# Regrouping the first MLP matmul, moving weight loads, and moving one layernorm from VectorE to ScalarE in a two-layer spectral and MLP kernel

## The chip, the cores and the metric

The kernel runs on one core of a Trainium2 chip. The metric is the time on the device in microseconds (us), as the median of several executions. The kernel before takes 796.93 us (5 runs, 795.81 to 799.64).

The engines are TensorE (PE in the profile, its weight loads PEld), VectorE (DVE), ScalarE (ACT), GpSimd (POOL), and SyncE (SP), which only issues transfers here. Each works through its own instructions in order.

## The reference, cut to what matters

```
def _A_ref(x, w_r, w_i):                     # spectral mixer, S = 2048, D = 576
    X = rfft2(x.astype(float32))             # over sequence and features
    return irfft2(X * (w_r + 1j * w_i), s=(S, D)).astype(bfloat16)

def _B_ref(x, w1, b1, w2, b2):               # MLP, F = 4608
    h = gelu(layernorm(x) @ w1 + b1)
    return h @ w2 + b2

x = A_x                                      # (1, 2048, 576) bf16
for _ in range(2):                           # two layers, same weights
    x = x + _A_ref(layernorm(x), A_w_r, A_w_i)
    x = x + _B_ref(layernorm(x), B_w1, B_b1, B_w2, B_b2)
```

## The kernel before

The Fourier transforms are matmuls with constant matrices. `x` stays in SBUF, the memory that the engines work from, as 16 tiles of 128 x 576. Matmuls write to PSUM; an *eviction* is the copy from PSUM to SBUF. Transforms of the layer's input come first (the change doesn't touch them), then these stages:

- **Inner stage** (`middle`): 16 steps of transform, multiplication by the spectral weights, and transform back. Each result `h` goes through an SBUF-to-SBUF transfer, the *exchange*, to other partitions. The next stage needs all 16 of them.
- **Output stage** (`spectral_out`): eight steps of two tiles. It also normalises and transposes ("turns") the first quad of four tiles for the MLP (`Prep`).
- **MLP**: four quads of four tiles. Each has a first matmul (`mlp_up`, with GELU) and a second one (`mlp_down`).

PSUM has three buffers of two banks (`big_ps`), handed out in turn. The parts that the change touches:

```
# inner stage: four buffers in turn for what the exchange sends
h = at(r_sb, [P, 2, KP], 592 * (10 + n % 4))
if n % 4 == 2: nc.vector.tensor_copy(out=h[:], in_=ph[:, :, 0:KP])
else:          nc.scalar.copy(out=h[:], in_=ph[:, :, 0:KP])
exchange(hx, E_ORDER[n], h)

# output stage
for n in range(9):
    if n < 8:
        idft_v(n)                 # 8 matmuls, then ScalarE evicts u2(n)
        if n % 2 == 0: idft_v_rest(n // 2)
    if n >= 1: idft_k(n - 1)      # two tiles: 6 matmuls each, 3 VectorE adds each
    if n == 2: prep.stats()       # VectorE statistics, ScalarE square root, VectorE reciprocal
    if 3 <= n < 7: prep.norm(n - 3)          # VectorE
    if 4 <= n < 8: prep.turn(n - 4, "act")   # 5 transposes, ScalarE eviction
    ...

# first MLP matmul: D = 576 is four 128-row pieces and one of 64 rows
for fg in range(0, NFC, 4):       # NFC = 36 chunks of 128 hidden features
    phs = [big_ps([P, 2, 512]) for _ in range(2)]
    for q in range(4):
        for ci in range(4):       # 16 full-height matmuls
            nc.tensor.matmul(phs[q // 2][:, q % 2, :], lhsT=w1_sb[...], rhs=yT[:, ci, :], start=(ci == 0), stop=False)
    for q in range(4):            # 4 half-height ones, two at a time in the two halves of the array
        rows = slice(64 * (q % 2), 64 * (q % 2) + 64)
        nc.tensor.matmul(phs[q // 2][:, q % 2, :], lhsT=w1r_sb[rows, ...], rhs=yT[rows, 4, :], start=False, stop=True)
    ...                           # four GELU evictions on ScalarE
```

In layer 1 the weights `w1` are loaded during the inner stage (three loads of 576 KB) and the output stage (the rest).

## Time and profile before

Stage lengths in the profiled execution run from a stage's first matmul to the next stage's first:

| Stage | Layer 1, us | Layer 2, us |
|---|---|---|
| inner | 33.19 | 29.52 |
| output | 33.52 | 33.36 |
| first MLP matmul, each of 4 passes | 36.86 | 36.86 to 36.88 |
| second MLP matmul, 4 passes | 41.16 to 52.13 | 35.45 to 36.41 |

The second MLP matmul of layer 1 is long because layer 2's input transforms run within it, and after it in its last pass (52.13 us).

The head of the page, three rows of busy time in 40 slices (tenths; PEclk is the TensorE clock that was granted, in tenths of full speed), and the chain of waits:

```profile
span 795.4 us, 12427 instructions
...
PE   8877799999999999999998787999999999999998
...
ACT  7944355433543354335423734552064125303610
...
PEclk9999899999999999999999998999999999999999
...
PE 79%; DVE 7%; issue 5%; DMA 4%; ACT 2%; POOL 1%; SPq 0%; POOLq 0%; ACTq 0%; DVEq 0%
```

TensorE is 79% of the chain. It has few gaps in the MLP passes; the sevens and eights are the spectral stages with their input transforms, and the two dips of the clock fall in the output stages.

The first MLP matmul, from the timeline of TensorE (start us, length us, engine, line, operation, count):

```profile
511.46 0.61 PE L529 MATMUL psb<-yT,w1r_sb 64*128 64x512 bf16 x4
512.00 3.63 PE L523 MATMUL psb<-yT,w_sb 128*128 128x512 bf16 x16
515.55 0.60 PE L529 MATMUL psb<-yT,w1r_sb 64*128 64x512 bf16 x4
516.09 0.39 PE L523 MATMUL psb<-yT,w_sb 128*128 128x512 bf16 x1
```

A group of four chunks repeats every 4.10 us. The starts of the single matmul records show where it goes:

```
full-height   515.028   515.243              steps of 0.216 us
half-height   515.555 (with 515.558)         0.312 after the last full-height one
half-height   515.782 (with 515.784)         0.227 later
full-height   516.093                        0.311 later
```

Each change between full and half height costs about 0.095 us on top of the 0.216 us that a matmul takes anyway.

Waits in layer 1's inner stage that end with a transfer (engine, line, waited-for: total us, times, longest):

```profile
ACT r_sb L407 <- DMA b_sb<-r_sb: 6.4, 6, 1.8
...
DVE r_sb L405 <- DMA b_sb<-r_sb: 2.6, 2, 1.4
```

L407 and L405 are the evictions into the four `h` buffers. They wait for the exchange to have read the buffer's old content.

Layer 2's output stage, from the timeline of ScalarE (in brackets: idle before, and what ended it), and, in the second fence, the longest of TensorE's waits there:

```profile
473.42 0.58 ACT L449 CAST u2r<-pss 34x512 bf16<-34x512 f32 x1
480.21 0.30 ACT L259 ACTIVATE sq<-mv,c_eps 128x4 f32<-128x4 f32 x1 [6.21 <-DVE mv L252]
480.53 1.01 ACT L436 CAST u<-psb 128x1024 bf16<-128x1024 f32 x1
```

```profile
PE psb L431 <- ACT u L436: 4.2, 1, 4.2
```

The square root (L259) stands in ScalarE's queue behind VectorE's statistics and holds up the eviction of `u` (L436) behind it; TensorE then waits 4.2 us for that PSUM buffer. The clock pays afterwards. The stretch from 480.3 to 487.1 (window and length; busy us of PE, PEld, DVE, ACT, POOL, with counts; granted clock; DMA):

```profile
480.30:487.10 6.80, 5.51 (x36) 3.53 (x36) 4.51 (x10) 3.31 (x5) 0.24 (x1) 0.50 0.01 2
```

The granted clock is 0.50. The Trainium skill (TensorE: Matmul & The Clock Gate, Part 1) says that TensorE's clock goes to half after an idle window of about 3.4 us. This trace agrees only in part: the half-clock stretch lasts 6.8 us, two such windows, but it begins 2.9 us into the gap of 4.2 us (477.40 to 481.59).

The four spectral stages in the same view, in order of time:

```profile
43.89:77.08 33.19, 23.71 (x143) 14.01 (x144) 23.59 (x69) 17.01 (x28) 6.01 (x10) 0.95 0.61 177
77.08:110.60 33.52, 26.60 (x244) 19.02 (x245) 26.35 (x60) 16.69 (x22) 5.36 (x11) 0.90 0.35 107
436.82:466.34 29.52, 22.29 (x143) 13.34 (x143) 23.12 (x68) 16.81 (x28) 1.25 (x2) 1.00 0.47 138
466.34:499.70 33.36, 26.53 (x244) 18.98 (x245) 26.26 (x60) 16.69 (x22) 0.94 (x4) 0.90 0.00 1
```

In the output stages (second and fourth line) VectorE is busy 26.3 us, ScalarE 16.7 us, and the clock is 0.90.

### The profile page before, as it was taken

How to read it: one execution, taken by the hardware profiler on the slowest of the kernel's cores; microseconds unless marked ns; L12 is line 12 of the kernel's file. 1: busy time of each engine (PE TensorE's matmuls, PEld its weight loads, DVE VectorE, ACT ScalarE, POOL GpSimd, SP SyncE). 2: the span in 40 equal slices, each digit the busy share in tenths (PEclk: the TensorE clock that was granted, in tenths of full speed). 3: DMA queues.
4: the chain of work that ended last, by engine and by line, in shares of the span. 5: the costliest groups of instructions: out<-in, count | busy, mean ns of one | idle time of the engine just before them, and what ended most of it. 6: DMA issues, size and time to landing. Idle time of an engine off the chain costs nothing.

```text
span 795.4 us, 12427 instructions
## 1 busy us (share of the span) xinstructions
PE 751.7 (95%) x5195; PEld 460.1 (58%) x5195; DVE 272.4 (34%) x865; ACT 330.5 (42%) x512; POOL 46.7 (6%) x89
## 2 busy tenths in 40 slices
PE   8877799999999999999998787999999999999998
PEld 5644553686368536863685545338735853684376
DVE  7765790136013601340142958601220140010011
ACT  7944355433543354335423734552064125303610
POOL 3220111000000000000004000100000000000000
PEclk9999899999999999999999998999999999999999
DMA  8855337000000000000004510430000000000000
GB/s 245 223 155 165 106 103 240 1 10 15 0 9 9 16 1 8 8 16 1 8 15 141 149 47 1 153 116 9 23 1 1 16 16 1 8 16 8 0 9 22
DMA packets 19079, 41.58 MB, mean 52 GB/s; under 512 B 1860, under 2 KB 12944, under 8 KB 19024
## 3 DMA queue, kind: packets, MB, share of 16 engines
q0 software_dynamic: 7040, 27.88, 11.6%
q1 hardware_dynamic: 11584, 12.46, 5.2%
q8 instruction: 40, 0.66, 0.3%
q10 hardware_dynamic: 400, 0.47, 0.2%
q14 instruction: 15, 0.12, 0.0%
HBM read 28.93 MB, written 2.36 MB: 39 GB/s over the span
## 4 chain that ended last, share of the span: by engine, by line
PE 79%; DVE 7%; issue 5%; DMA 4%; ACT 2%; POOL 1%; SPq 0%; POOLq 0%; ACTq 0%; DVEq 0%
PE psb L551 35%; PE psb L523 32%; PE psb L529 5%; DMA b_sb<-r_sb 2%; PE psb L309 2%; DVE tt L467 1%; PE psb L461 1%; PE psb L431 1%; POOL h_sb L201 1%; PE pss L510 1%; DVE x_sb L468 1%; PE pss L299 1%; ACT u L436 1%; DMA h_sb<-const_i 1%; DVE x_sb L469 1%
## 5 line engine op out<-in xcount | busy, mean ns | idle before, releaser
L523 PE MATMUL psb<-yT,w_sb 128*128 128x512 bf16 x1152 | 261.0, 380 | 1.3 <-DVE x_sb L469 1.3
L536 ACT ACTIVATE h_sb<-psb,b_sb 128x512 bf16<-128x512 f32 x288 | 174.5, 688 | 200.9 <-PE psb L529 200.9
L551 PEld LDWEIGHTS <-h_sb 128*128 128x128 bf16 x2304 | 223.2, 98 | 58.2 <-issue 3.4
L523 PEld LDWEIGHTS <-w_sb 128*128 128x128 bf16 x1152 | 107.3, 98 | 148.3 <-issue 28.1
L551 PE MATMUL psb<-r_sb,h_sb 128*128 128x288 bf16 x1280 | 168.9, 286 | 0.0
L551 PE MATMUL psb<-v_sb,h_sb 128*128 128x288 bf16 x1024 | 133.7, 286 | 0.0
L559 DVE TENSOR_TENSOR x_sb<-psb,xb 128x576 bf16<-128x576 f32 x32 | 24.2, 758 | 260.5 <-PE psb L551 260.5
L500 DVE TENSOR_SCALAR xn<-x_sb,mv,rs 128x576 bf16<-128x576 bf16 x32 | 12.8, 426 | 198.4 <-PE pss L510 141.1
L251 DVE BATCH_NORM_STATS2 stats<-x_sb 128x6 f32<-128x288 bf16 x128 | 50.9, 440 | 0.0
L512 ACT COPY yT<-pss 128x640 bf16<-128x640 bf16 x32 | 22.2, 692 | 65.0 <-PE pss L510 65.0
L301 ACT COPY xT<-pss 96x768 bf16<-96x768 bf16 x32 | 25.2, 788 | 45.0 <-PE pss L299 45.0
L529 PE MATMUL psb<-yT,w1r_sb 64*128 64x512 bf16 x288 | 43.6, 381 | 0.0
L314 ACT ACTIVATE z<-psb,rs 128x580 bf16<-128x580 f32 x32 | 29.5, 921 | 20.8 <-PE psb L309 20.5
L503 POOL COPY xn<-xn 128x64 bf16<-128x64 bf16 x32 | 7.6, 248 | 426.5 <-DVE xn L500 351.2
L467 DVE TENSOR_TENSOR tt<-psb,x_sb 128x576 f32<-128x576 f32 x32 | 24.0, 750 | 20.7 <-PE psb L461 20.7
L309 PE MATMUL psb<-c_fd,xT 96*128 96x290 bf16 x192 | 30.1, 292 | 0.5 <-ACT y L330 0.4
L461 PE MATMUL psb<-c_gd,u 128*128 128x288 bf16 x128 | 27.2, 306 | 3.3 <-ACT u L436 1.7
L330 ACT CAST y<-psb 128x580 bf16<-128x580 f32 x24 | 15.4, 640 | 32.3 <-PE psb L327 32.3
L378 ACT CAST r_sb<-psb 128x580 bf16<-128x580 f32 x32 | 20.4, 643 | 20.0 <-PE psb L376 9.8
L402 PE MATMUL psb<-r_sb,h_sb 128*128 128x290 bf16 x128 | 21.9, 291 | 7.1 <-DVE r_sb L390 3.9
L529 PEld LDWEIGHTS <-w1r_sb 64*128 64x128 bf16 x288 | 8.2, 94 | 30.5 <-issue 30.5
L547 DVE TENSOR_TENSOR xb<-x_sb,b_bc 128x576 f32<-128x576 bf16 x32 | 24.0, 749 | 0.0
(80 smaller groups left out, 534.2 us busy)
## 6 DMA issues: line engine op xcount, KB each, us to landing
r_sb<-in_B_w_dram POOLq DMA_DIRECT2D x4, 1440.0 KB, 7.4
w_sb<-in_B_w_dram POOLq DMA_DIRECT2D x8, 576.0 KB, 5.4
v_sb<-in_B_w_dram POOLq DMA_DIRECT2D x4, 1152.0 KB, 6.8
h_sb<-const_i POOLq DMA_DIRECT2D x8, 384.0 KB, 6.0
v_sb<-y SPq DMA_DIRECT2D x16, 145.0 KB
b_sb<-r_sb SPq DMA_DIRECT2D x16, 145.0 KB
b_sb<-y SPq DMA_DIRECT2D x16, 145.0 KB
v_sb<-r_sb SPq DMA_DIRECT2D x16, 145.0 KB
```

The lines of the kernel that those rows point to most:

```text
L251: nc.vector.bn_stats(out=stats[:, h, :], in_=x_sb[:, t, h * DH : (h + 1) * DH])
L301: marks["turn", t] = nc.scalar.copy(out=xT[:], in_=pt[0:96]).ins
L309: nc.tensor.matmul(pz[:, o, 0:KP], lhsT=xT[:, 3 * o + ci, :], rhs=c_fd[:, 3 * o + ci, :], start=(ci == 0), stop=(ci == 2),)
L314: nc.scalar.activation(out=z[:].rearrange("p r (j o) -> p r o j", o=2), in_=pz[:, :, 0:KP].rearrange("p o (r j) -> p r o j", r=2), func=AC ...
L461: nc.tensor.matmul(po[:, o, 0:DH], lhsT=lhsT, rhs=c_gd[0 : (98 if q == 2 else 128), 3 * o + q, :], start=(q == 0), stop=(q == 2),)
L467: nc.vector.tensor_tensor(out=tt[:], in0=po[:, 0:1, 0:DH].to_broadcast([P, 2, DH]), in1=xr, op=ALU.add)
L523: nc.tensor.matmul(phs[q // 2][:, q % 2, :], lhsT=w1_sb[:, ci, (fg + q) * 128 : (fg + q + 1) * 128], rhs=yT[:, ci, :], start=(ci == 0), st ...
L529: nc.tensor.matmul(phs[q // 2][:, q % 2, :], lhsT=w1r_sb[rows, (fg + q) // 2, :], rhs=yT[rows, 4, :], start=False, stop=True,)
L536: marks["ht", fc] = nc.scalar.activation(out=ht[:], in_=phs[q // 2][:, q % 2, :], func=ACT.Gelu_apprx_tanh, bias=b1_sb[:, fc : fc + 1], sc ...
L547: nc.vector.tensor_tensor(out=xb[:], in0=xr, in1=b2_bc[:].rearrange("p (h n) -> p h n", h=2), op=ALU.add)
L551: nc.tensor.matmul(po[:, h, 0:DH], lhsT=hts[fc][:, i * 128 : (i + 1) * 128], rhs=w2_chunk[fc][:, h * DH : (h + 1) * DH], start=(fc == 0), ...
L559: nc.vector.tensor_tensor(out=xr, in0=po[:, :, 0:DH], in1=xb[:], op=ALU.add)
```

## The change

It has three parts, each for one stage:

1. **First MLP matmul.** Six chunks share one visit to half-height mode instead of four. The third pair of chunks starts its sum with the half-height matmuls and adds the full-height ones afterwards. All three PSUM buffers are used.
2. **Inner stage.** Nine `h` buffers instead of four, and in layer 1 three `w1` loads move into the output stage.
3. **Output stage.** Statistics and norms of the first quad go from VectorE to ScalarE, spread over more steps. The sums of `x` and of its square come from two ScalarE passes per tile with an accumulator output. The turns come later.

```diff
-            h = at(r_sb, [P, 2, KP], 592 * (10 + n % 4))
+            h = at(r_sb, [P, 2, KP], 592 * (10 + n % 9))
 [...]
-            if n == 2:
-                prep.stats()
-            if 3 <= n < 7:
-                prep.norm(n - 3)
-            if 4 <= n < 8:
-                prep.turn(n - 4, "act")
+            if n == 2:
+                prep.stats_act((0, 1))
+            if n == 3:
+                prep.stats_act((2, 3))
+            if n == 4:
+                prep.scale_act()
+            for i in {5: (0, 1), 6: (2,), 7: (3,)}.get(n, ()):
+                prep.norm_act(i)
+            for i in {6: (0,), 7: (1, 2), 8: (3,)}.get(n, ()):
+                prep.turn(i, "act")
 [...]
+        def stats_act(self, tiles):
+            [...]
+            for i in tiles:
+                t = self.quad[i]
+                for k, func in enumerate((ACT.Copy, ACT.Square)):
+                    nc.scalar.activation(out=at(h_sb, [P, D], 512 * 34), in_=x_sb[:, t, :], func=func, accum_out=sums[:, k, i : i + 1])
+        def scale_act(self):
+            [... mean and variance from the sums: three small VectorE operations ...]
+            nc.scalar.activation(out=var[:], in_=var[:], func=ACT.Sqrt, bias=c_eps[:, 1:2], scale=1.0 + EPS)
+            nc.vector.reciprocal(out=rs[:], in_=var[:])
+            [... shift = -mean * rs ...]
+        def norm_act(self, i):
+            [...]
+            nc.scalar.activation(
+                out=xn[:, 0:D], in_=x_sb[:, self.quad[i], :], func=ACT.Identity, bias=shift[:, i : i + 1], scale=rs[:, i : i + 1]
+            )
+            nc.gpsimd.tensor_copy(out=xn[:, D:640], in_=xn[:, D - 64 : D])
 [... mlp_up: the old loop over groups of four is replaced by: ...]
+        for p in range(0, NFC // 2, 3):          # p counts pairs of chunks
+            for k in range(2):
+                acc[p + k] = big_ps([P, 2, 512])
+                full(p + k, True)                # 8 full-height matmuls, start the sum
+            acc[p + 2] = big_ps([P, 2, 512])
+            for k in range(3):
+                rest(p + k, k == 2)              # 2 half-height ones; they start the third pair's sum
+            gelu(p)
+            gelu(p + 1)
+            full(p + 2, False)                   # end the third pair's sum
+            gelu(p + 2)
 [... loads of layer 1, inner stage ...]
-                6: [lambda b: load_w1(0, 0, b)],
-                8: [lambda b: load_w1(1, 0, b)],
-                10: [lambda b: load_w1(2, 0, b)],
 [... loads of layer 1, output stage ...]
-                1: [lambda: load_w1(3, 0, t0), lambda: load_w1r(0, t0), lambda: load_w1r(1, t0)],
+                0: [lambda: load_w1(0, 0, ("u2", 0)), lambda: load_w1(1, 0, ("u2", 0))],
+                1: [lambda: load_w1(2, 0, t0), lambda: load_w1(3, 0, t0)],
+                2: [lambda: load_w1r(0, t0), lambda: load_w1r(1, t0)],
```

More of the change, by code (lines that the diff above doesn't have):

```diff
@@ L402, in idft_c @@
                     nc.tensor.matmul(ph[:, o, 0:KP], lhsT=i1[:, n % 4, pl, :], rhs=xp[:, ri, :], start=(q == 0), stop=(q == 1))
-            h = at(r_sb, [P, 2, KP], 592 * (10 + n % 4))
+            h = at(r_sb, [P, 2, KP], 592 * (10 + n % 9))
             if n % 4 == 2:
-                nc.vector.tensor_copy(out=h[:], in_=ph[:, :, 0:KP])
+                ins = nc.vector.tensor_copy(out=h[:], in_=ph[:, :, 0:KP]).ins
             else:
-                nc.scalar.copy(out=h[:], in_=ph[:, :, 0:KP])
+                ins = nc.scalar.copy(out=h[:], in_=ph[:, :, 0:KP]).ins
+            marks["h", n] = ins
             exchange(hx, E_ORDER[n], h)
@@ L435, in idft_v @@
             u2 = work.tile([P, 2, 2, 2, 128], BF16, tag="turn")
-            nc.scalar.copy(out=u2[:], in_=pu[:])
+            marks["u2", n] = nc.scalar.copy(out=u2[:], in_=pu[:]).ins
             st["u2", n] = u2
@@ L491, in __init__ @@
             self.quad, self.st, self.sqrt = QUADS[q], {}, sqrt
+        def stats_act(self, tiles):
+            if 0 in tiles:
+                self.sums = work.tile([P, 2, 4], F32, tag="ln_sums", name=f"sums{uid()}")
+            sums = self.sums
+            for i in tiles:
+                t = self.quad[i]
+                for k, func in enumerate((ACT.Copy, ACT.Square)):
+                    nc.scalar.activation(out=at(h_sb, [P, D], 512 * 34), in_=x_sb[:, t, :], func=func, accum_out=sums[:, k, i : i + 1])
+            self.sums = sums
+        def scale_act(self):
+            s1, s2 = self.sums[:, 0], self.sums[:, 1]
+            mean = work.tile([P, 4], F32, tag="ln_hv")
+            var = work.tile([P, 4], F32, tag="ln_v")
+            rs = work.tile([P, 4], F32, tag="ln_rs", bufs=4)
+            shift = work.tile([P, 4], F32, tag="ln_t")
+            nc.vector.tensor_scalar(out=mean[:], in0=s1, scalar1=1.0 / D, scalar2=None, op0=ALU.mult)
+            nc.vector.tensor_mul(out=shift[:], in0=mean[:], in1=mean[:])
+            nc.vector.scalar_tensor_tensor(out=var[:], in0=s2, scalar=1.0 / D, in1=shift[:], op0=ALU.mult, op1=ALU.subtract)
+            nc.scalar.activation(out=var[:], in_=var[:], func=ACT.Sqrt, bias=c_eps[:, 1:2], scale=1.0 + EPS)
+            nc.vector.reciprocal(out=rs[:], in_=var[:])
+            nc.vector.scalar_tensor_tensor(out=shift[:], in0=mean[:], scalar=-1.0, in1=rs[:], op0=ALU.mult, op1=ALU.mult)
+            self.rs_shift = rs, shift
+            self.yT = work.tile([P, 5, 512], BF16, tag="yT", bufs=1, name=f"yT{uid()}")
+        def norm_act(self, i):
+            rs, shift = self.rs_shift
+            xn = work.tile([P, 640], BF16, tag="xn", bufs=3)
+            nc.scalar.activation(
+                out=xn[:, 0:D], in_=x_sb[:, self.quad[i], :], func=ACT.Identity, bias=shift[:, i : i + 1], scale=rs[:, i : i + 1]
+            )
+            nc.gpsimd.tensor_copy(out=xn[:, D:640], in_=xn[:, D - 64 : D])
+            self.st[i] = xn
         def stats(self):
@@ L518, in mlp_up, with full, rest, gelu @@
         loads = list(loads)
-        for fg in range(0, NFC, 4):
-            phs = [big_ps([P, 2, 512]) for _ in range(2)]
-            for q in range(4):
+        acc = {}
+        def full(p, first):
+            ph = acc[p]
+            for q in range(2):
+                fc = 2 * p + q
                 for ci in range(4):
                     nc.tensor.matmul(
-                        phs[q // 2][:, q % 2, :], lhsT=w1_sb[:, ci, (fg + q) * 128 : (fg + q + 1) * 128], rhs=yT[:, ci, :],
-                        start=(ci == 0), stop=False,
-                    )
-            for q in range(4):
-                rows = slice(64 * (q % 2), 64 * (q % 2) + 64)
-                nc.tensor.matmul(
-                    phs[q // 2][:, q % 2, :], lhsT=w1r_sb[rows, (fg + q) // 2, :], rhs=yT[rows, 4, :],
-                    start=False, stop=True,
-                )
-            for q in range(4):
-                fc = fg + q
+                        ph[:, q, :], lhsT=w1_sb[:, ci, fc * 128 : (fc + 1) * 128], rhs=yT[:, ci, :],
+                        start=(first and ci == 0), stop=(not first and ci == 3),
+                    )
+        def rest(p, first):
+            for q in range(2):
+                rows = slice(64 * q, 64 * q + 64)
+                nc.tensor.matmul(acc[p][:, q, :], lhsT=w1r_sb[rows, p, :], rhs=yT[rows, 4, :], start=first, stop=not first)
+        def gelu(p):
+            for q in range(2):
+                fc = 2 * p + q
                 ht = at(h_sb, [P, 512], 512 * fc)
                 marks["ht", fc] = nc.scalar.activation(
-                    out=ht[:], in_=phs[q // 2][:, q % 2, :], func=ACT.Gelu_apprx_tanh, bias=b1_sb[:, fc : fc + 1], scale=1.0
+                    out=ht[:], in_=acc[p][:, q, :], func=ACT.Gelu_apprx_tanh, bias=b1_sb[:, fc : fc + 1], scale=1.0
                 ).ins
                 hts.append(ht)
+        for p in range(0, NFC // 2, 3):
[9 more added lines that the diff above has]
+            gelu(p + 2)
             if loads:
-                loads.pop(0)(("ht", fg))
+                loads.pop(0)(("ht", 2 * p))
         return hts
```

## The prediction

> **What bounds it now.** The chain of waits is 79% TensorE: the eight MLP passes (first matmul 32%, second 35%) run back to back at granted clock 1.00. The spectral stages do not. In the table of busy time by stretch, layer 1's inner transforms take 33.5 us (43.5 to 77.0), layer 2's only 29.8; each spectral output stage takes 33.4 us with TensorE busy 26.5 us, VectorE 26.3 us, ScalarE 16.7 us, and clock 0.90.
>
> **1. MLP first matmul (eight passes of nine groups).** In the timeline a group of four chunks takes 4.096 us: 18 matmul slots of 0.2158 us = 3.884, the rest is the step from full-height to half-height matmuls (0.312 instead of 0.216 us, so 0.096 lost), the step back (0.095), and about 0.02 of small gaps. The Trainium skill (TensorEngine Tiling, Key Properties) says that a change of tiling mode drains TensorE; this trace agrees, about 0.095 us each. The change makes six groups of six chunks: 27 x 0.2158 + about 0.22 = 6.05 us, 36.3 instead of 36.9 us a pass. All of it is critical: 8 x 0.56 = **4.5 us**. The third PSUM buffer should cause no waits: GELUs start every 0.605 us, so a buffer is free about 0.8 us before it is needed.
>
> **2. Layer 1's inner transforms.** Evictions and VectorE copies there wait for the exchange transfers (waits: 6.4 + 2.6 us, landing up to 7 us late), since w1 loads share the DMA engines and only four buffers exist. Nine buffers and no w1 loads remove both. VectorE then paces it as in layer 2 (1.31 us an iteration, about 0.7 more in every fourth; last eviction to next matmul 3.1 us): out stage starts near 73.3 instead of 77.1: **3.7 us**. Layer 2's inner transforms do not change.
>
> **3. Spectral output, both layers.** VectorE needs 1.52 us per tile; the next matmul's PSUM buffer needs 14 tiles, 21.3 us. Before, it also does statistics (3.85 us) and four norms (1.8 us), and ScalarE's square root waits in order for the statistics (idle until 480.2), holding the next eviction and TensorE for 4 us; the clock then falls to half for 6.8 us (480.3 to 487.1). Moving the work to ScalarE adds there eight passes of 128x576 (estimate 0.65 us each, from the 0.54 us spacing of 128x580 evictions plus bias pointer), four norms (about 0.8), and delays evictions. The Trainium skill (ScalarE: Activation LUTs, What ACT_TABLE_LOAD costs) gives about 93 ns for each pointer operand. Working through the new order with these durations, the first MLP matmul comes about 28.5 us after the stage's start, not 33.4, provided that the clock stays full: 4.7 us each, **9.4 us** in all. No table load is added. w1's loads, now in this stage, need about 21 us from its start and are there in time.
>
> Sum 17.6 us: **779.5 us**, range 774.5 to 786.5. Faster by over 2%: 0.60; within 2%: 0.39; slower: 0.01.
>
> **What shows it.** Six half-height matmuls in a row and 36.3 us a pass; no waits of evictions for the exchange in layer 1; output stages of about 28.7 us with ScalarE busier than 24 us, VectorE below 23 us, and clock near 1.0.
>
> **What would make it wrong.** Accumulating activations that cost far more than 0.65 us, or the strict order on ScalarE holding evictions, so that the output stage gains under 3 us; half clock staying; w1 arriving late for the first MLP pass; exchange transfers still backlogged at the end of layer 1's inner transforms by the remaining loads.

## The result, and the profile after

The changed kernel takes 781.83 us (8 runs, 780.94 to 784.01). The kernel before took 797.54 us in the same rounds and those above (15 runs). The ratio is 0.9807, with a 95% interval of 0.9794 to 0.9821. A ratio is the mean time of one kernel's fast runs over that of the other's of the same rounds, so it is not quite the ratio of the medians. The change is worth 1.9%; the interval straddles the 2% line, so whether it is "faster by over 2%" stays unclear.

The page's head, the same rows and the chain:

```profile
span 779.6 us, 12441 instructions
...
PE   8877899999999999999998787999999999999998
...
ACT  7954865324542454236323658551164126303600
...
PEclk9999999999999999999999999999999999999999
...
PE 81%; DVE 5%; ACT 5%; issue 5%; DMA 3%; POOL 1%; SPq 0%; ACTq 0%; POOLq 0%; DVEq 0%
```

In this execution the clock no longer dips, and ScalarE's share of the chain has grown from 2% to 5%. The span went from 795.4 to 779.6 us; the stages account for the 15.8 us:

| Stage | Before, us | After, us | Difference | Predicted |
|---|---|---|---|---|
| first MLP matmul, sum of 8 passes | 294.9 | 289.9 | -5.0 | -4.5 |
| inner, layer 1 | 33.19 | 30.01 | -3.2 | -3.7 |
| output, layer 1 | 33.52 | 29.57 | -3.95 | -4.7 |
| output, layer 2 | 33.36 | 29.57 | -3.8 | -4.7 |
| inner, layer 2 | 29.52 | 29.70 | +0.2 | 0 |
| all else | | | -0.05 | 0 |

First MLP matmul, timeline of TensorE: the group of six repeats every 6.04 us (490.77 to 496.81), with one visit to half height:

```profile
490.02 0.82 PE L573 MATMUL psb<-yT,w1r_sb 64*128 64x512 bf16 x6
490.77 5.35 PE L565 MATMUL psb<-yT,w_sb 128*128 128x512 bf16 x24
496.06 0.82 PE L573 MATMUL psb<-yT,w1r_sb 64*128 64x512 bf16 x6
496.81 0.82 PE L565 MATMUL psb<-yT,w_sb 128*128 128x512 bf16 x3
```

In layer 1's inner stage no eviction waits for the exchange any more, and no matmul of the MLP pass behind it waits for `w1`. The four spectral stages in order of time, columns as before:

```profile
44.08:74.09 30.01, 22.58 (x143) 13.36 (x144) 23.32 (x69) 16.81 (x28) 4.41 (x7) 1.00 0.46 137
74.09:103.66 29.57, 24.18 (x245) 17.89 (x246) 23.17 (x50) 24.25 (x42) 6.94 (x14) 1.00 0.57 181
427.20:456.90 29.70, 22.45 (x142) 13.33 (x143) 23.21 (x68) 16.81 (x28) 1.40 (x2) 1.00 0.48 140
456.90:486.47 29.57, 24.18 (x244) 17.89 (x245) 23.17 (x50) 24.26 (x42) 0.95 (x4) 1.00 0.00 1
```

In the output stages ScalarE rose from 16.7 to 24.3 us, VectorE fell from 26.3 to 23.2 us, and the clock is 1.00. ScalarE's timeline there, layer 2:

```profile
464.59 0.68 ACT L505 ACTIVATE h_sb<-x_sb 128x576 bf16<-128x576 bf16 x1
465.18 0.19 ACT L505 ACTIVATION_READ_ACCUMULATOR h_sb<-x_sb 128x1 f32 x1
465.39 0.68 ACT L505 ACTIVATE h_sb<-x_sb 128x576 bf16<-128x576 bf16 x1
...
472.72 1.17 ACT L450 CAST u2r<-pss 34x512 bf16<-34x512 f32 x2
475.06 0.30 ACT L517 ACTIVATE var<-var,c_eps 128x4 f32<-128x4 f32 x1 [1.18 <-DVE var L516]
475.38 1.01 ACT L437 CAST u<-psb 128x1024 bf16<-128x1024 f32 x1
```

Two things are new. Each statistics pass is followed by a separate instruction that reads the accumulator, and passes start 0.81 us apart (464.586, 465.393 in single records), where the prediction estimated 0.65. And the square root still makes ScalarE idle in front of an eviction, for 1.18 us instead of 6.21.

### The profile page after: what moved, and what is told of

Read it like the earlier page. It is cut to its first block, busy times and chain, and to the rows that moved or that the text cites. A ratio compares the mean times of both kernels' runs of the same rounds, so it can differ in the third digit from the quotient of the medians.

```text
span 779.6 us, 12441 instructions
## 1 busy us (share of the span) xinstructions
PE 741.3 (95%) x5195; PEld 461.4 (59%) x5195; DVE 263.5 (34%) x841; ACT 345.1 (44%) x552; POOL 46.6 (6%) x89
## 4 chain that ended last, share of the span: by engine, by line
PE 81%; DVE 5%; ACT 5%; issue 5%; DMA 3%; POOL 1%; SPq 0%; ACTq 0%; POOLq 0%; DVEq 0%
PE psb L606 36%; PE psb L565 33%; PE psb L573 5%; PE psb L309 2%; ACT u L437 1%; PE psb L462 1%; PE pss L549 1%; DVE r_sb L389 1%; DVE r_sb L388 1%; PE pss L299 1%; ACT u2r L450 1%; PE psb L432 1%; DMA h_sb<-const_i 1%; DVE r_sb L390 1%; POOL h_sb L201 1%
## 5 line engine op out<-in xcount | busy, mean ns | idle before, releaser
L565 PE MATMUL psb<-yT,w_sb 128*128 128x512 bf16 x1152 | 258.3, 380 | 1.6 <-ACT yT L551 1.6
L579 ACT ACTIVATE h_sb<-psb,b_sb 128x512 bf16<-128x512 f32 x288 | 171.6, 695 | 189.1 <-PE psb L573 189.1
L539 DVE TENSOR_SCALAR xn<-x_sb,mv,rs 128x576 bf16<-128x576 bf16 x24 | 9.4, 427 | 197.2 <-PE pss L549 141.1
L251 DVE BATCH_NORM_STATS2 stats<-x_sb 128x6 f32<-128x288 bf16 x112 | 44.7, 441 | 0.0
L573 PE MATMUL psb<-yT,w1r_sb 64*128 64x512 bf16 x288 | 39.5, 380 | 0.0
L462 PE MATMUL psb<-c_gd,u 128*128 128x288 bf16 x128 | 24.9, 286 | 3.0 <-ACT u L437 1.6
L542 POOL COPY xn<-xn 128x64 bf16<-128x64 bf16 x24 | 5.8, 252 | 335.2 <-DVE xn L539 335.0
L573 PEld LDWEIGHTS <-w1r_sb 64*128 64x128 bf16 x288 | 10.2, 94 | 26.0 <-issue 20.3
```

The costliest lines, as they stand in the source:

```text
L251: nc.vector.bn_stats(out=stats[:, h, :], in_=x_sb[:, t, h * DH : (h + 1) * DH])
L462: nc.tensor.matmul(po[:, o, 0:DH], lhsT=lhsT, rhs=c_gd[0 : (98 if q == 2 else 128), 3 * o + q, :], start=(q == 0), stop=(q == 2),)
L565: nc.tensor.matmul(ph[:, q, :], lhsT=w1_sb[:, ci, fc * 128 : (fc + 1) * 128], rhs=yT[:, ci, :], start=(first and ci == 0), stop=(not first ...
L573: nc.tensor.matmul(acc[p][:, q, :], lhsT=w1r_sb[rows, p, :], rhs=yT[rows, 4, :], start=first, stop=not first)
L579: marks["ht", fc] = nc.scalar.activation(out=ht[:], in_=acc[p][:, q, :], func=ACT.Gelu_apprx_tanh, bias=b1_sb[:, fc : fc + 1], scale=1.0).ins
```

## The experiments

Twelve kernels ran, three rounds each (the last one five). All were marked correct. Stage lengths are from the profiled execution of each run, measured as above; times are medians.

### One visit to half height per pair of chunks

```diff
-        for p in range(0, NFC // 2, 3):  [... groups of three pairs ...]
+        for p in range(NFC // 2):
+            acc[p] = big_ps([P, 2, 512])
+            full(p, True)
+            rest(p, False)
+            gelu(p)
```

> The changed kernel, but each pair of chunks runs its two half-height matmuls right after its own eight full-height ones: 18 trips into half-height mode a pass instead of 6, three PSUM buffers still in turn. Theory (each step between the modes costs about 0.095 us): a pass takes 18 x (9 x 0.2158 + about 0.21) = 38.7 us instead of 36.24, so about +20 us, 801 to 803 us in all. Rival (the gain of the new loop came from the third PSUM buffer or from evictions spread out, not from fewer mode changes): passes stay near 36.2 us and the total near 782 us.

Measured: 801.92 us; every pass takes 38.77 to 38.78 us. Twelve more visits cost 38.78 - 36.24 = 2.54 us, or 0.21 us a visit: the two steps of 0.095 us and about 0.02 of small gaps. The kernel before, with nine visits, fits the same line: 36.24 + 3 x 0.21 = 36.87 us against 36.86. So the buffers gave nothing by themselves, and the theory holds.

### The new matmul loop alone

The kernel before, with the new `mlp_up` and nothing else.

> The kernel before with the new loop of the first MLP matmul and nothing else. Theory (the parts of the change act in different stages and add up): 8 x 0.62 = 5.0 us less than before, 792 to 793 us, all other stages as before. Rival (the parts help one another, for example by shifting loads): a different amount, or other stages that move by over 0.5 us.

Measured: 792.68 us against 798.06 us of the kernel before in the same rounds. Every pass takes 36.24 or 36.25 us; inner stages 33.09 and 29.52 us, output stages 33.65 and 33.05 us. The other stages stay within 0.35 us, so this part acts by itself, as the theory says.

### Four exchange buffers, loads moved

```diff
-            h = at(r_sb, [P, 2, KP], 592 * (10 + n % 9))
+            h = at(r_sb, [P, 2, KP], 592 * (10 + n % 4))
```

> The changed kernel with four exchange buffers again, w1's loads still moved out. Theory (the loads were the cause, the buffers only cushion): layer 1's inner stage takes 30.0 to 31.0 us, total at most 1 us above the changed kernel; some short waits of evictions for the exchange return. Rival (the buffers were the cause): the stage goes back to about 33 us, total 785 us.

### Nine exchange buffers, loads back in the inner stage

```diff
+                6: [lambda b: load_w1(0, 0, b)],
+                8: [lambda b: load_w1(1, 0, b)],
+                10: [lambda b: load_w1(2, 0, b)],
 [... and the output stage's first loads as in the kernel before ...]
```

> The changed kernel with nine exchange buffers, but the three w1 loads back in layer 1's inner stage. Theory (the DMA engines are shared, so the exchange itself is late whatever the buffers): no eviction waits for the exchange, yet the output stage waits at its start for the last transfers; the stage takes 32 to 33 us, total about 784.5 us. Rival (buffers alone suffice): stage near 30 us, total near 782 us.

Measured for these two: 782.54 and 784.61 us; layer 1's inner stage 30.61 and 32.02 us (changed kernel: 30.01). A wait from each one's layer 1, the first from the four-buffer run, the second from the run with early loads:

```profile
ACT r_sb L407 <- DMA b_sb<-r_sb: 2.0, 2, 1.5
```

```profile
PE psb L432 <- DMA b_sb<-r_sb: 3.0, 1, 3.0
```

With four buffers some eviction waits come back, but they cost just 0.6 us of the stage. With early loads no eviction waits; the delay moves to the stage's end, where the output stage's first matmul (L432) waits 3.0 us for the last transfers. More buffers let the engines run ahead of a late transfer; they do not make it arrive. The early loads also cost 1.0 us in layer 1's output stage (30.61 us, clock 0.94 in the view of busy time). Both theories hold. So of about 3.2 us in the inner stage, 2.0 hang on the loads, given nine buffers, and 0.6 on the buffers, given the moved loads; together they give more than the sum, since each alone hides part of the other's cost (counted from the kernel before: loads alone 2.6, buffers alone 1.2). Differences of 0.3 us in this stage mean nothing: in six of the runs that leave it as changed it took 30.3 to 30.4 us at a clock of 0.94, in the others 30.0 at 1.00.

### The old preparation in the changed kernel

The calls of `prep` in the output stage are those of the kernel before.

> The changed kernel with the old preparation of the first quad in the output stage: statistics and norms on VectorE, square root on ScalarE in the third step. Theory (parts add up): each output stage goes back to about 33.4 us, with half clock for one stretch in each, total about 789.5 us. Rival (the gain came from elsewhere in the stage, such as the loads moved into it or the later turns): less than 5 us more than the changed kernel.

### The same, with TensorE kept busy through the gap

```diff
+            if n == 3:
+                keep_busy(16)      # 16 matmuls of zeros into a spare PSUM tile
```

> As the run before, with sixteen matmuls of zeros (about 3.5 us) put into TensorE's idle stretch behind the third step, so that the clock isn't halved. It tells how much of the gain was the clock. My estimate from the half-clock stretch of the kernel before: about 2 us a stage, so stages of 31.4 us and a total of about 785.5 us, clock near 1.0. Rival (the clock cost nothing, since VectorE paces the stage): stages stay at 33.4 us, total 789.5 us.

Measured for these two: 788.62 and 785.67 us. Their output stages of layers 1 and 2, first without and then with the matmuls of zeros:

```profile
73.94:107.59 33.65, 26.73 (x245) 19.16 (x245) 26.41 (x60) 16.69 (x22) 6.97 (x14) 0.90 0.49 159
...
460.67:493.74 33.07, 26.23 (x245) 18.85 (x245) 26.23 (x60) 16.69 (x22) 0.95 (x4) 0.90 0.00 1
```

```profile
74.84:106.00 31.16, 27.83 (x262) 19.17 (x262) 26.27 (x60) 16.66 (x22) 6.97 (x14) 1.00 0.53 172
...
459.16:490.23 31.07, 27.82 (x261) 19.15 (x261) 26.18 (x60) 16.67 (x22) 0.95 (x4) 1.00 0.01 2
```

The first shows that the third part, its later turns included, is worth 4.1 and 3.5 us a stage (33.65 and 33.07 against 29.57), as the theory says. The second shows that more than half of this is the clock: sixteen matmuls of zeros alone take 2.5 and 2.0 us off, with VectorE and ScalarE doing what they did before. Moving the work, its new order and the later turns add the other 1.5 to 1.6 us; no run here separates these three.

### The old engines, with the new order

```diff
-                prep.stats_act((0, 1))       [... n == 2, and (2, 3) at n == 3 ...]
+                prep.bn((0, 1))              # VectorE statistics of two tiles
-                prep.scale_act()             [... n == 4 ...]
+                prep.scale()                 # square root on ScalarE, reciprocal on VectorE
-                prep.norm_act(i)
+                prep.norm(i)                 # VectorE
```

> The changed kernel with statistics and norms on VectorE as before, but spread in time as in the change (two tiles a step, square root in the fifth step, norms and turns one step later each). It removes the blocking of ScalarE without moving work off VectorE. Theory (both count: VectorE then has 21.3 us of tiles, 3.9 of statistics, 1.8 of norms behind a start of 3.9): stages of about 31.2 us, total about 785. Rival 1 (only the blocking counted): stages of 29.6 us, total 782. Rival 2 (only VectorE's load counted): stages near 33 us, total 789.

Measured: 789.0 us, the runs spread from 786.78 to 792.16; output stages 32.07 and 32.20 us. It does not separate the reasons as planned: the granted clock fell here too (0.95 in both output stages: half clock for 3.41 us at the end of a gap of 2.23 us in TensorE's work), and one pass of the first MLP matmul behind it took 37.86 instead of 36.24 us. Nor did the edit remove the blocking, as it was meant to: ScalarE still idled 3.3 us for the square root's input (6.2 before, 1.2 in the changed kernel), and TensorE waited 2.2 us for the eviction behind it. It does show that spreading the work without taking it off VectorE (busy 27.5 us) falls short of the changed kernel by 2.5 us a stage. How much of that is load, how much blocking and how much clock stays open.

### Statistics passes without the sums

```diff
-  nc.scalar.activation(out=..., in_=x_sb[:, t, :], func=func, accum_out=sums[:, k, i : i + 1])
+  nc.scalar.activation(out=..., in_=x_sb[:, t, :], func=func)      # sums set to 1.0 once
```

> The changed kernel without the accumulator outputs of the eight statistics passes (the sums are a constant, so the result is wrong on purpose). The trace of the changed kernel has a separate read of the accumulator of 0.187 us after each pass, and passes 0.81 us apart instead of the estimated 0.65. Theory (this is the term that was mis-sized): passes about 0.58 us apart, output stages shorter by 0.9 us or more, so 28.7 us or less, total 780 or less. Rival (the miss comes from the order on ScalarE elsewhere, and the passes have slack): stages within 0.3 us of 29.57.

Measured: 780.90 us; output stages 29.13 us. Half of what the theory asked for and more than the rival's 0.3, so neither holds as stated. Passes are 0.715 us apart (in single records), not 0.58. The run was marked correct although the sums are a constant: this comparison hardly notices the norm of one quad, so it is no proof that a preparation is right.

### Norms on GpSimd

```diff
-            nc.scalar.activation(out=xn[:, 0:D], ..., func=ACT.Identity, bias=shift[...], scale=rs[...])
+            nc.gpsimd.tensor_scalar(out=xn[:, 0:D], ..., scalar1=rs[...], scalar2=shift[...], op0=ALU.mult, op1=ALU.add)
```

> The changed kernel with the first quad's four norms on GpSimd instead of ScalarE. ScalarE loses four passes of about 0.87 us in the output stage. Theory (ScalarE's queue is what holds the stage after the change): stages of about 28.5 us, total about 780, if a GpSimd norm takes near 1 us (not measured yet). Rival (the stage hangs on VectorE and the matmul order, or GpSimd is too slow and the turns wait for it): 29.5 us or more.

### The square root behind the next eviction

The root and its two VectorE follow-ups are issued after `idft_v(5)`, not at the end of the step before.

> The changed kernel with the square root behind the next eviction on ScalarE. In the trace of the changed kernel ScalarE is free from about 473.9 and waits for the root's input until 475.06, and only then evicts. Theory (strict order on ScalarE is still a cost, the rest of the miss): the eviction comes 0.9 us or more sooner, stages shorter by 0.3 to 0.9 us (28.7 to 29.3). Rival (VectorE's queue paces that stretch, so nothing is gained): 29.5 to 29.6.

### Four scratch tiles

```diff
-  out=at(h_sb, [P, D], 512 * 34)
+  out=at(h_sb, [P, D], 512 * 31 + D * (2 * (i % 2) + k))
```

> The changed kernel with four scratch tiles for the statistics passes instead of one; the sums are right. The run without sums still had passes 0.715 us apart, each with a wait on ScalarE's own earlier pass, where an estimate from 128x580 evictions gives about 0.57. Theory (the common scratch tile makes each pass wait for the one before): the first four passes come 0.70 us apart with their accumulator reads instead of 0.81, stages shorter by 0.1 to 0.4 us. Rival (the accumulator reads alone set the distance): no change in distance or stage.

Measured for these three: 780.90, 781.27 and 780.55 us; output stages of layers 1 and 2 are 29.24 and 29.05, 29.09 and 29.14, 29.15 and 29.14 us. Three different cuts each give 0.3 to 0.5 us. The theories of the moved root and of the scratch tiles hold. The GpSimd norms take 3.4 us off ScalarE and yet give no more than the others; their theory asked for 1 us. ScalarE's timeline with four scratch tiles:

```profile
464.71 0.68 ACT L505 ACTIVATE h_sb<-x_sb 128x576 bf16<-128x576 bf16 x1
465.30 0.18 ACT L505 ACTIVATION_READ_ACCUMULATOR h_sb<-x_sb 128x1 f32 x1
465.39 0.67 ACT L505 ACTIVATE h_sb<-x_sb 128x576 bf16<-128x576 bf16 x1
465.97 0.19 ACT L505 ACTIVATION_READ_ACCUMULATOR h_sb<-x_sb 128x1 f32 x1
466.06 0.67 ACT L505 ACTIVATE h_sb<-x_sb 128x576 bf16<-128x576 bf16 x1
```

The passes now start 0.67 us apart, accumulator reads included. With one scratch tile each pass carried a wait for ScalarE's own step before it (the accumulator read, or the pass itself in the run without sums); that cost 0.14 us a pass.

### All of it together

Norms on GpSimd, four scratch tiles, the root behind the next eviction with its follow-ups between two tiles of VectorE, and the last turn ahead of the last tiles' matmuls:

```diff
+            if n == 5: prep.root_act()                  # right after idft_v(5)
+            if n == 8: prep.turn(3, "act")
             if n >= 1:
-                idft_k(n - 1)
+                idft_k(n - 1, prep.root_dve if n == 5 else None)   # called between the two tiles
```

> The changed kernel with what the last runs point to together: norms on GpSimd, four scratch tiles, square root behind the next eviction with its two VectorE follow-ups between two tiles, and the last turn ahead of the last tile's matmuls. In the run with GpSimd norms VectorE still waited 1.3 us for delayed evictions, 0.35 us for the root, and the last turn cost 0.8 us after VectorE's fourteenth tile. Theory (single fixes stopped at 29.1 us because these waits are in series and each run took away only one): output stages of 27.3 to 27.9 us, total about 778. Rival (another limit, such as the matmul order, holds the stage at 29.1): stages of 28.8 us or more, total 780 or more.

Measured: 778.15 us (777.36 to 779.71) against 797.40 us of the kernel before in the same rounds, ratio 0.9761 with an interval of 0.9746 to 0.9776. The output stages:

```profile
73.77:101.64 27.87, 24.16 (x245) 17.80 (x245) 22.19 (x48) 21.12 (x38) 10.23 (x18) 1.00 0.61 192
455.18:482.44 27.26, 24.14 (x245) 17.89 (x245) 21.80 (x48) 21.12 (x38) 4.14 (x8) 1.00 0.00 1
```

The single fixes had stopped near 29.1 us; together they reach 27.9 and 27.3 us. This beats both kernels. It supports the picture of waits in series on a path that passes through ScalarE, TensorE and VectorE in turn. The three single gains add up to 1.2 and 1.4 us of the 1.7 and 2.3 that the combined run gains on the changed kernel. The rest belongs to the two edits that were never run alone (the follow-ups between two tiles, the last turn moved ahead) or to the interplay; no run separates these.

## Why the prediction was right, and where it was off

The time, 781.83 us, lies in the stated range of 774.5 to 786.5; the sum of 17.6 us was 1.8 us too large. The first two misses cancel each other; the rest is the output stages.

- **First MLP matmul, 4.5 us predicted, 5.0 measured.** The mechanism is shown by the run with one visit per pair: 0.21 us a visit. The size was short because a group of six takes 6.04 us, not "6.05", and 36.24 us a pass against 36.86 makes 0.62, not 0.56. The "0.605 us" between GELU starts is a stretch of four divided by four; in single records they start 0.57 to 0.59 us apart, which leaves more room. No waits for the third buffer appeared, as foreseen.
- **Inner stage of layer 1, 3.7 predicted, 3.2 measured.** Shared transfers were the cause, as the runs with early loads and with four buffers show. The output stage began at 74.09, not "near 73.3". The larger part of that miss is the term "last eviction to next matmul 3.1 us": it was 3.58 us here, and 3.43 in layer 2 of the kernel before already.
- **Output stages, 9.4 predicted, 7.7 measured.** The step that was off is "eight passes of 128x576 (estimate 0.65 us each)": they took 0.81. The run with four scratch tiles brought them to 0.67 and the stage down by 0.43 us: the wait at the common scratch tile was the main term left out (0.14 us a pass). That 0.67 is so near to 0.65 is luck. The estimate counted a bias pointer (about 0.09) that the passes don't have (the profile lists `x_sb` as their one input) and left out the accumulator read, which adds about as much: without it, and still with the wait, passes were 0.715 apart instead of 0.81. The four norms, "about 0.8", started 0.77 us apart where two followed each other. The prediction named "the strict order on ScalarE holding evictions" as a risk; the run with the root moved shows that it cost another 0.4 to 0.5 us. These two come to about 0.9 us together, which is the size of the miss per stage. That they would simply add is only argued; the last run did both among other edits.
- **The clock.** The prediction made full clock a condition and did not price it apart. It is the larger share: 2.0 to 2.5 us of about 3.8 a stage, by the run with matmuls of zeros. So more than half of the gain in these stages came through what the prediction took as a condition, and not through the work moved off VectorE.
- **ScalarE busier than 24 us and clock near 1.0** came true (24.3 us, 1.00). VectorE "below 23 us" was missed narrowly at 23.2, and stages of "about 28.7" came at 29.57.

## What to carry to other kernels

Count the trips between array modes and the idle gaps of TensorE, not only its busy time: a trip cost 0.21 us here, and a gap of 4.2 us cost another 2 us through the clock, which sixteen dummy matmuls bought back in one run. When work moves to an engine that also evicts PSUM, look for what its strict order now holds up, and give passes whose output nobody reads more than one scratch tile. When several single fixes all stop at the same time, try them together before concluding that none matters: here three single gains added up to more than half of the combined one.

## What the Trainium skill lacked or had wrong

- **TensorEngine Tiling (Array Packing), Key Properties**, says that switching the tiling mode drains TensorE but not for how long. Here a step between 128-row and 64-row mode costs about 0.095 us, and a visit 0.21 us (38.78 against 36.24 us for twelve more visits).
- **ScalarE: Activation LUTs** says that an ACTIVATE can give an accumulator output, but not its cost. Here it is a separate instruction, ACTIVATION_READ_ACCUMULATOR, of 0.187 us, which overlaps the pass before it by about 0.09 us; passes with it start 0.67 us apart.
- **The same page, What ACT_TABLE_LOAD costs**, says that back-to-back ACTIVATEs overlap by about 93 ns. No overlap between passes was left where each wrote the same scratch tile: passes of 0.683 us started 0.715 us apart even without accumulator reads. Its figure for two pointer operands (186 + 480 + 2 x 93 = 852 ns for 576 elements) agrees with this trace's norms, 868 ns.
- **TensorE: Matmul & The Clock Gate**, Part 1, has the clock go to half after an idle window of about 3.4 us. Here less was enough: half clock began 2.9 us into the gap of 4.2 us, and at the end of a gap of 2.23 us in the run with the old engines in the new order (then clock 0.50 for 3.41 us). None of the pages read here prices the aftermath for a stage that TensorE does not bound: 2.0 to 2.5 us.
- **GPSIMD Engine Reference**, Elementwise, has costs for fp32 operations and loops, none for a bf16 pass with two per-partition scalars. On 128x576 it took 0.82 us (four of them, 3.3 us busy), against 0.87 us on ScalarE; with the copy of the tail in between, they started 1.09 us apart.
